# DeltaNet and SwiGLU on one core: scores leave PSUM through two engines, their mask moves to the unit's slot, and the plan is re-timed

## The chip, the core and the metric

The kernel runs on one core of a Trainium2 chip. A core has a matrix engine (TensorE, PE in the profile, with its weight loads shown as PEld), a vector engine (VectorE, DVE), a scalar engine (ScalarE, ACT), GpSimd (POOL) and SyncE (SP), which here only issues DMAs. Each engine takes its instructions strictly in the order of the program; engines wait for each other, and for DMAs, on semaphores. Matmul results land in PSUM, from which only DVE and ACT read here. The metric is the time of one execution on the device in microseconds, and the time before is the median of four runs.

## The reference: what is computed

Two blocks follow each other. The first is a DeltaNet recurrence over 768 steps for 4 batches of 8 heads with head dimension 48; the second is an RMS norm and a SwiGLU feed-forward block over the 3,072 resulting tokens, with 384 model columns and 1,536 hidden columns:

```python
k_n = k / (np.linalg.norm(k, axis=-1, keepdims=True) + 1e-06)
for t in range(S):
    y[:, :, t] = np.einsum('bhd,bhde->bhe', q[:, :, t], state)
    v_old = np.einsum('bhde,bhd->bhe', state, kt)
    state = state + bt[:, :, :, None] * np.einsum('bhd,bhe->bhde', kt, vt - v_old)
...
rms = np.sqrt(np.mean(x * x, axis=-1, keepdims=True) + 1e-06)
xn = x / rms * rms_g
g = xn @ w_gate
silu = g * (1.0 / (1.0 + np.exp(-g)))
val = xn @ w_val
return (silu * val @ w_out).astype(np.float32)
```

Within a chunk of 128 steps the recurrence becomes a triangular system: scores of keys against keys, and of keys against queries (masked to the earlier steps), an inverse of a unit triangular matrix, and products with the state. The weights arrive as 64-bit floats and the kernel makes 32-bit floats of them itself.

## The kernel before, in words

**Units.** A unit `n` is one chunk of 128 steps of one batch with its 8 heads: 6 chunks by 4 batches give 24 units, units 0 to 3 being chunk 0. The FFN works on pairs of units, 256 tokens, in a pass (`ffn`, L1018) of 12 steps; a step multiplies gate and value (`p_gv`, L1037), takes `sil` on ACT (L1046) and `h_f` on DVE (L1049), and `leave` (L1022) adds the step's product to the output accumulators `p_o` (L1024). The first two pairs run as four half passes of 6 steps.

**The start.** `begin` (L1087) loads keys and queries, scores the keys of chunk 0 (`score_part`, `keep_keys`), sends the diagonal 32 by 32 blocks through DRAM into the layout of the inversion (`gather_two`, tile `gd`, then `gblk`), scores the queries (the Q phase), and inverts on DVE (`invert_halves`). The result goes through DRAM again (`td`, then `tt`). `stay_warm` issues matmuls whose result nobody reads. `fetch` loads one tile of weights (two DMAs), `shrink` and `convert` (ACT L251; DVE L261 to L292) turn weight tiles into 32-bit floats, five DVE steps for each of 18 tiles; `convert_rest` spreads what is left over the first FFN passes.

**Chunks 1 to 5.** `prepare(n)` normalizes the keys, transposes queries and keys on PE, copies them out (`kqt`, ACT L408), scores both (`score`, L411, four PSUM tiles `p_g`), evacuates the scores into `gp`, and sends the diagonal blocks to DRAM (`gather`, L445). Each of the four `p_g` tiles is evacuated by two ACT copies (`keys`, L428 and L429) and two DVE multiplications by the causal mask (`queries`, L433); both engines write into the same `gp` rows, and the DVE of a tile stands behind its ACT copies. `invert(g)` (L599) runs 31 steps of two DVE instructions (L618, L627) over a chunk or a pair of units. `slot(v, z, y)` (L965) runs the products of up to three units at different stages: `corner`, `inner`, `outer`, `scale`, `transpose_y`.

**PSUM.** Eight buffers: two for `p_gv`, two for `p_o` and the filler, and four (`ps_delta`, L76) that everything else takes in turn. A transpose or a score right behind a score therefore waits until a `p_g` tile is evacuated.

**Order.** There is no automatic scheduler: pieces are generators that yield plan times, `run_plan` (L1078) always advances the one with the earliest time, and the order of the calls is the order on every engine's queue. One plan unit is half an FFN step on PE (6 of the traced matmuls, 1.3 us). The plan's constants stand at the end (L1134 to L1162). SP's queue holds most loads and the output; ACT's queue holds the gathers of `gd`, so that ACT does nothing else while a gather waits for `gp`. `scale_v` multiplies the values of a unit by the key norms on GpSimd.

## Time and profile before

| | before |
|---|---|
| median of 4 runs (lowest to highest) | 857.9 us (854.65 to 859.13) |
| the profiled execution, its time | 859.13 us |
| its span, first to last instruction | 857.4 us |
| PE / DVE / ACT / POOL busy in the span | 816.3 / 497.9 / 247.7 / 111.9 us |
| granted TensorE clock, mean | 0.974 |

The profiled execution is the slowest of the four. The span is cut below into five stretches by what PE does: up to 40.66 us the start, to 67.61 us chunk 0 alone, to 201.9 us the first FFN steps with weight conversion, preparation and inversion of chunk 1, to 342 us chunk 1's slots and chunk 2's inversion, and from there the steady part, in which PE is never without work. A busy PE is a modelled figure: a matmul at half clock counts as busy too.

### The profile page before, as it was taken

Reading aid. Unit: us, or ns where it says so; the run is one execution under the profiler, and the core shown is the slowest. Engines: PE = TensorE matmul, PEld = TensorE weight load, DVE = VectorE, ACT = ScalarE, POOL = GpSimd, SP = SyncE. Lnnn points to the kernel's source line nnn. Section 1 sums busy time; section 2 is a strip of 40 time slices with the busy share of each in tenths; the row PEclk is TensorE's granted clock in tenths of the full one; section 3 lists DMA queues with packets and bytes.
Section 4 is the critical chain, followed back from the end, with each engine's and each line's share of the span. In section 5 each row is a group of like instructions: output and inputs, shape, how many; then the busy total and the mean of one; then the engine's idle time right before and its main releaser. Section 6 shows DMA issues by size and latency. Waiting matters only on the chain.

```text
span 857.4 us, 20449 instructions
## 1 busy us (share of the span) xinstructions
PE 816.3 (95%) x8628; PEld 629.3 (73%) x8628; DVE 497.9 (58%) x1233; ACT 247.7 (29%) x655; POOL 111.9 (13%) x154
## 2 busy tenths in 40 slices
PE   7898978889999989999999999999999999999998
PEld 6586756666777766777778777777778777877776
DVE  7868968793344865755856756856756841211100
ACT  5333545201443141233132142142142121220101
POOL 6003332200113020020020020020020000000000
PEclk9959989899999999999999999999999999999999
DMA  6846335104232042133042051051032020000000
GB/s 153 233 101 222 114 109 162 36 0 105 49 69 65 1 101 48 21 69 75 2 89 55 2 105 39 2 105 40 9 79 39 2 63 1 2 20 1 19 1 18
DMA packets 152204, 52.03 MB, mean 61 GB/s; under 512 B 143760, under 2 KB 146832, under 8 KB 152112
## 3 DMA queue, kind: packets, MB, share of 16 engines
q1 hardware_dynamic: 124960, 36.95, 18.9%
q0 software_dynamic: 2080, 10.23, 3.4%
q10 hardware_dynamic: 25072, 3.54, 2.5%
q8 instruction: 68, 1.11, 0.5%
q14 instruction: 24, 0.20, 0.1%
HBM read 36.54 MB, written 14.16 MB: 59 GB/s over the span
## 4 chain that ended last, share of the span: by engine, by line
PE 68%; DVE 7%; DMA 2%; ACT 2%; SPq 1%; issue 1%; ACTq 1%; DVEq 0%
PE p_gv L1037 36%; PE p_o L1024 18%; DVE tmp L618 3%; DVE ttb L627 2%; PE p_y L781 2%; PE p_g L419 2%; PE p_k L819 2%; PE p_y L819 2%; PE p_z L841 2%; PE p_t L403 1%; DMA gblk<-gd 1%; PE p_v L688 1%; DMA gd<-gp 1%; DVE h_f L1049 1%; ACT gp L428 1%
## 5 line engine op out<-in xcount | busy, mean ns | idle before, releaser
L1037 PE MATMUL p_gv<-xt,wgv_sb 128*128 128x256 f32 x1728 | 414.2, 386 | 1.3 <-DVE xt L1008 0.7
L1037 PEld LDWEIGHTS p_gv<-xt,wgv_sb 128*128 128x128 f32 x1728 | 322.7, 192 | 64.1 <-issue 4.0
L1024 PE MATMUL p_o<-wo_sb,h_f 128*128 128x384 f32 x576 | 215.8, 499 | 9.6 <-DVE h_f L1049 9.5
L1024 PEld LDWEIGHTS p_o<-wo_sb,h_f 128*128 128x128 f32 x576 | 107.6, 193 | 61.0 <-DVE h_f L1049 14.0
L1046 ACT ACTIVATE sil<-p_gv 128x256 f32<-128x256 f32 x144 | 55.2, 383 | 336.1 <-PE p_gv L1037 316.5
L1049 DVE TENSOR_TENSOR h_f<-sil,p_gv 128x256 f32<-128x256 f32 x144 | 60.0, 417 | 153.2 <-ACT sil L1046 152.0
L618 DVE SCALAR_TENSOR_TENSOR tmp<-gblk,nbeta,ttb 64x112 f32<-64x112 f32 (+27 forms) x248 | 101.2, 408 | 29.5 <-DMA gblk<-gd 21.7
L627 DVE TENSOR_TENSOR ttb<-ttb,tmp 64x112 f32<-64x112 f32 (+27 forms) x248 | 86.6, 349 | 8.5
L433 DVE TENSOR_TENSOR gp<-p_g,mask 64x128 f32<-64x128 f32 (+1 forms) x160 | 37.9, 277 | 47.3 <-ACT gp L429 43.2
L993 POOL TENSOR_SCALAR ms<-ms 128x1 f32<-128x1 f32 x24 | 6.2, 259 | 447.0 <-ACT y L985 446.7
L338 POOL TENSOR_TENSOR knrm<-ksum,half 128x8 f32<-128x8 f32 x24 | 41.2, 1717 | 166.2 <-DVE ksum L337 166.0
L408 ACT COPY kqt<-p_t 128x512 f32<-128x512 f32 x48 | 28.0, 584 | 41.0 <-PE p_t L403 29.1
L419 PE MATMUL p_g<-kqt 64*64 64x192 f32 x640 | 32.1, 329 | 4.4 <-ACT kqt L408 2.4
L841 PEld LDWEIGHTS p_z<-v_raw,tt 64*64 64x64 f32 x768 | 25.9, 142 | 9.4 <-issue 6.8
L419 PEld LDWEIGHTS p_g<-kqt 64*64 64x64 f32 x640 | 22.7, 132 | 13.6 <-issue 5.9
L985 ACT ACTIVATE y<-p_y 128x384 f32<-128x384 f32 x24 | 11.8, 490 | 67.6 <-PE p_y L781 67.6
L841 PE MATMUL p_z<-v_raw,tt 64*64 64x48 f32 x768 | 28.8, 227 | 1.4 <-ACT sil L1046 1.4
L708 ACT COPY vs<-p_v 32x256 f32<-32x256 f32 x48 | 17.4, 362 | 42.2 <-PE p_w L695 37.9
L859 PE MATMUL p_x<-tt,gp 64*64 64x64 f32 x384 | 28.8, 229 | 0.0
L781 PE MATMUL p_y<-u,gp 128*64 128x48 f32 x768 | 27.7, 229 | 0.0
L781 PEld LDWEIGHTS p_y<-u,gp 128*64 128x64 f32 x768 | 26.4, 145 | 1.4 <-issue 1.4
L428 ACT COPY gp<-p_g 128x128 f32<-128x128 f32 x80 | 21.2, 265 | 16.1 <-PE p_g L419 14.5
(128 smaller groups left out, 808.7 us busy)
## 6 DMA issues: line engine op xcount, KB each, us to landing
kpad<-in_k_dram SPq DMA_DIRECT2D x24, 192.0 KB, 2.8
qpad<-in_q_dram SPq DMA_DIRECT2D x24, 192.0 KB, 3.2
v_raw<-in_v_dram SPq DMA_DIRECT2D x24, 192.0 KB, 3.6
out_dram<-o_sb SPq DMA_DIRECT2D x24, 192.0 KB, 2.0
raw<-in_moe_w_val_dram POOLq DMA_DIRECT2D x8, 384.0 KB, 4.0
raw<-in_moe_w_out_dram POOLq DMA_DIRECT2D x8, 384.0 KB, 4.1
gd<-gp ACTq DMA_DIRECT2D x80, 32.0 KB, 2.1
tt<-td SPq DMA_DIRECT2D x80, 32.0 KB, 2.1
```

The lines of the kernel that those rows point to most:

```text
L338: nc.gpsimd.tensor_tensor(out=norms[c][:, b * H : (b + 1) * H], in0=ksum, in1=half, op=ALU.pow)
L419: nc.tensor.matmul(to, pair[d, K1 if i else K0], pair[d, places], skip_group_check=True)
L433: nc.vector.tensor_tensor(out=to[p, :, place], in0=p_g[p, :, place], in1=mask[p, i, None].to_broadcast([p.stop, 2, HC]), op=ALU.mult,)
L618: nc.vector.scalar_tensor_tensor(out=tmp, in0=gblk[p, i, None, i + 1 :].to_broadcast(shape), scalar=nbeta[p, i : i + 1], in1=ttb[p, 0 : i ...
L627: nc.vector.tensor_tensor(out=to, in0=to, in1=tmp, op=ALU.add)
L781: nc.tensor.matmul(p_y[p, h], gp[i][:, h, HC * place : HC * (place + 1)], u[:, h], start=(n_y < B and h == 0), stop=True, skip_group_check ...
L819: nc.tensor.matmul(p_o[p, 2 * j : 2 * j + 2].rearrange("p h d -> p (h d)"), kq[:, j, place], st[:, j], start=(alone or j == 0), stop=alone ...
L841: nc.tensor.matmul(p_z[p, h], tt[n_z % B][p, h], r[p, h], start=(h == 0), stop=(p is lo or n_z >= B), skip_group_check=True,)
L1024: nc.tensor.matmul(p_o[i], h_f[:, i * C : (i + 1) * C], wo_sb[:, f], start=(f == f0), stop=(f == f1 - 1),)
L1037: nc.tensor.matmul(p_gv[:, i], wgv_sb[:, i * KT + t, f * 128 : (f + 1) * 128], xt[:, t], start=(t == 0), stop=(t == KT - 1),)
L1046: nc.scalar.activation(out=sil, in_=p_gv[:, 0], func=ACTF.Silu)
L1049: nc.vector.tensor_tensor(out=h_f, in0=sil, in1=p_gv[:, 1], op=ALU.mult)
```

## The change

- **Scores.** `score` no longer takes an evacuation function. Each `p_g` tile is emptied by one engine alone with two plain copies (`leave`, 64 partitions by 384 numbers): the tiles of heads 0 to 3 by ACT, those of heads 4 to 7 by DVE, alternating. No mask is applied there.
- **Mask.** `mask_queries(n)` (two DVE instructions on `gp`, 64 by 512) now runs for every unit, in `slot` after `corner`; for units 2 and 3 it moves from the start of `first_chunk` to behind `inner`.
- **Blocks.** The 80 gathers of `gd` in `gather` are issued by SP instead of ACT.
- **Values.** `scale_v` for units 2 and 3 and for chunk 1 runs on ACT as 8 multiplications for each unit, at the unit's slot; chunk 2 and later stay on GpSimd.
- **Start.** In `begin`, the key norm's DVE part comes after the key copies, unit 3's copies are all on ACT, the first `shrink` and `convert` move into the Q phase behind its first transpose, and one weight tile fewer is fetched there; it is fetched behind `read_two(0)`.
- **FFN pass ends.** The last `leave` of a pass is yielded 2.5 plan units later instead of 0.9, behind the first matmuls of the next pass.
- **Other.** `transpose_y` of units 2 and 3 leaves PSUM through ACT (three multiplications) instead of DVE (one), `norm_k` in `prepare` moves one yield later, and the plan's times are re-set: preparation of chunk 1 from 8 + 4.5 b to 12.4 + 3.4 b with shorter yields, `invert(1)` from 33.5 with 0.62 a step to 30.4 with 0.68, slots 0.7 to 3 units later, `invert(2)` with 0.7 a step instead of 0.58.

```diff
@@ -385,6 +385,10 @@
 
     def scale_v(n, engine=nc.gpsimd):
         c, b = divmod(n, B)
+        if engine is nc.scalar:
+            for h in range(H):
+                nc.scalar.mul(vraw[n][:, h], vraw[n][:, h], norms[c][:, b * H + h : b * H + h + 1])
+            return
         engine.tensor_tensor(
             out=vraw[n],
             in0=vraw[n],
@@ -407,8 +411,12 @@
             )
         nc.scalar.copy(kqt[place_of(n)][:, :, place::2], p_t)
 
-
-    def score(n, groups, evacuate):
+    def leave(to, p_g, copy):
+        copy(out=to[lo, :, Q0:K1], in_=p_g[lo, :, Q0:K1])
+        copy(out=to[hi, :, K0:], in_=p_g[hi, :, K0:])
+
+
+    def score(n, groups):
         b = place_of(n)
         p_gs = [[ps_delta([128, 2, 4, HC], "p_g") for par in range(2)] for g in range(NP // 2)]
         for j in range(NP):
@@ -419,27 +427,10 @@
                 nc.tensor.matmul(
                     to, pair[d, K1 if i else K0], pair[d, places], skip_group_check=True
                 )
-        for g in range(NP // 2):
-            for par in range(2):
+        for par in range(2):
+            for g in range(NP // 2):
                 to = gp[b][:, 4 * g + par : 4 * g + 4 : 2].rearrange("p h (a t) -> p h a t", a=4)
-                evacuate(to, p_gs[g][par])
-
-    def keys(to, p_g):
-        nc.scalar.copy(to[:, :, K0], p_g[:, :, K0])
-        nc.scalar.copy(to[hi, :, K1], p_g[hi, :, K1])
-
-    def queries(to, p_g):
-        for place, p, i in ((Q0, lo, 0), (Q1, slice(0, C), 1)):
-            nc.vector.tensor_tensor(
-                out=to[p, :, place],
-                in0=p_g[p, :, place],
-                in1=mask[p, i, None].to_broadcast([p.stop, 2, HC]),
-                op=ALU.mult,
-            )
-
-    def both(to, p_g):
-        keys(to, p_g)
-        queries(to, p_g)
+                leave(to, p_gs[g][par], nc.vector.tensor_copy if g else nc.scalar.copy)
 
 
     def gather(n, size):
@@ -448,7 +439,7 @@
             gds[n // size] = dram.tile([NBLK * size * H, W, W], FP32, name=f"gd{size}")
         for a in range(NBLK):
             o, first = diagonal(a), (a * size + i) * H
-            nc.scalar.dma_start(
+            nc.sync.dma_start(
                 out=gds[n // size][first : first + H].rearrange("h r j -> r h j"),
                 in_=gp[place_of(n)][W * a : W * (a + 1), :, o : o + W],
             )
@@ -481,15 +472,16 @@
         return [(0, a), (1, b), (0, b), (1, a)]
 
     def prepare(n, size, dts):
-        norm_k(n, square_k(n, nc.scalar))
+        ksq = square_k(n, nc.scalar)
         yield dts[0]
+        norm_k(n, ksq)
         transpose(n, qpad[n % 2], Q0)
         if n + 2 < NU:
             load_q(n + 2)
         yield dts[1]
         transpose(n, kpad[n % NK], K0)
         yield dts[2]
-        score(n, crossed((0, slice(0, 3)), (1, slice(1, 4))), both)
+        score(n, crossed((0, slice(0, 3)), (1, slice(1, 4))))
         yield dts[3]
         gather(n, size)
         if n % size == size - 1:
@@ -518,11 +510,11 @@
     def heads(n, par, place):
         return gp[n][:, par::2, HC * place : HC * (place + 1)]
 
-    def keep_keys(n, p_gs):
+    def keep_keys(n, p_gs, copy=nc.vector.tensor_copy):
         for par in range(2):
             nc.scalar.copy(heads(n, par, K0)[lo], p_gs[par][lo, :, 0])
             own = gp[n][hi, par::2].rearrange("p h (a t) -> p h a t", a=4)
-            nc.vector.tensor_copy(out=own[:, :, K0::2], in_=p_gs[par][hi])
+            copy(out=own[:, :, K0::2], in_=p_gs[par][hi])
 
     def keep_queries(n, p_gs):
         for par in range(2):
@@ -531,7 +523,7 @@
 
     def mask_queries(n):
         for place, p in ((Q0, lo), (Q1, hi)):
-            part = gp[n][p, :, HC * place : HC * (place + 1)]
+            part = gp[place_of(n)][p, :, HC * place : HC * (place + 1)]
             nc.vector.tensor_tensor(
                 out=part, in0=part, in1=mask[p, place // 2, None].to_broadcast([HC, H, HC]), op=ALU.mult
             )
@@ -603,7 +595,7 @@
         if size == B:
             yield 1.5
             turn_beta(g)
-            for n in range(B * g, B * (g + 1)):
+            for n in range(B * g, B * (g + 1)) if g > 1 else ():
                 scale_v(n)
         else:
             apart = split_beta(g)
@@ -919,15 +911,12 @@
         yield
         update(0)
         load_k(B + 1)
-        scale_v(2)
-        scale_v(3)
-        mask_queries(2)
         yield dt
         update(1)
         reload()
         yield dt
         next(halved[2])
-        mask_queries(3)
+        scale_v(2, nc.scalar)
         yield dt
         next(halved[3])
         yield dt
@@ -935,6 +924,7 @@
         yield dt
         corner(2, None)
         next(halved[3])
+        scale_v(3, nc.scalar)
         yield dt
         corner(3, 2)
         yield dt
@@ -944,16 +934,18 @@
         inner(2, None, 3)
         yield dt
         inner(3, 2, None)
+        mask_queries(2)
         yield dt
         outer(None, 2)
         yield dt
         inner(None, 3, None)
+        mask_queries(3)
         yield dt
         outer(None, 3)
         yield dt
-        transpose_y(2, scale(*ys.pop(2)))
-        yield dt
-        transpose_y(3, scale(*ys.pop(3)))
+        transpose_y(2, scale(*ys.pop(2)), nc.scalar)
+        yield dt
+        transpose_y(3, scale(*ys.pop(3)), nc.scalar)
         yield dt
         update(2)
         yield dt
@@ -963,10 +955,12 @@
 
 
     def slot(v, z, y, dts):
-        if have(v) and v >= 3 * B:
-            scale_v(v)
+        if have(v) and not 2 * B <= v < 3 * B:
+            scale_v(v, nc.scalar if v < 2 * B else nc.gpsimd)
         if have(v) or have(z):
             corner(v, z)
+        if have(v):
+            mask_queries(v)
         yield dts[0]
         inner(z, y, z)
         yield dts[1]
@@ -998,19 +992,21 @@
         nc.scalar.mul(y, p_y.rearrange("p h d -> p (h d)"), rs)
         return y
 
-    def transpose_y(n, y):
+    def transpose_y(n, y, engine=nc.vector):
         if n % 2 == 0:
             xts[n // 2] = work.tile([128, KT, TOK], FP32, name="xt")
         o = C * (n % 2)
         p_xt = ps_delta([128, KT, 128], "p_xt")
         for t in range(KT):
             nc.tensor.transpose(p_xt[:, t], y[:, t * 128 : (t + 1) * 128], ident)
-        nc.vector.tensor_tensor(
-            out=xts[n // 2][:, :, o : o + C],
-            in0=p_xt,
-            in1=g_sb[:, :, None].to_broadcast([128, KT, 128]),
-            op=ALU.mult,
-        )
+        xt = xts[n // 2][:, :, o : o + C]
+        if engine is nc.scalar:
+            for t in range(KT):
+                nc.scalar.mul(xt[:, t], p_xt[:, t], g_sb[:, t : t + 1])
+        else:
+            nc.vector.tensor_tensor(
+                out=xt, in0=p_xt, in1=g_sb[:, :, None].to_broadcast([128, KT, 128]), op=ALU.mult
+            )
 
     halves = {}
 
@@ -1051,7 +1047,8 @@
                 leave(f - 1, last)
                 yield 1
             last = h_f
-        yield 0.9
+
+        yield 2.5
         leave(f1 - 1, last)
         for i in range(2):
             n = 2 * m + i
@@ -1091,16 +1088,16 @@
         transpose(0, kpad[0], K0)
         for n in range(B):
             if n + 1 < B:
-                norm_k(n + 1, square_k(n + 1, nc.vector))
+                ksq = square_k(n + 1, nc.vector)
                 transpose(n + 1, kpad[n + 1], K0)
             if n == 2:
                 gather_two(0)
                 turn_all_beta()
-            keep_keys(n, score_part(n, K0))
+            keep_keys(n, score_part(n, K0), nc.scalar.copy if n == 3 else nc.vector.tensor_copy)
+            if n + 1 < B:
+                norm_k(n + 1, ksq)
         gather_two(2)
         scale_beta(0, B)
-        tops.append(shrink(raws[0]))
-        convert(2)
         clear_ttb()
         for t in state + [ne]:
             nc.gpsimd.memset(t, 0.0)
@@ -1110,9 +1107,12 @@
                 turn_beta(0)
                 convert(3)
             transpose(n, qpad[n % 2], Q0)
+            if n == 0:
+                tops.append(shrink(raws[0]))
+                convert(2)
             stay_warm(2)
             load_q(n + 2)
-            if n < 3:
+            if n < 2:
                 fetch(nc.sync.dma_start)
             if n < 2:
                 load_v(n)
@@ -1120,6 +1120,7 @@
         tops.append(shrink(raws[1]))
         inverses = invert_halves()
         read_two(0, *inverses)
+        fetch(nc.sync.dma_start)
         stay_warm(4)
         stay_warm(8, ttb_all[:, 0:DM].rearrange("p (t m) -> p t m", m=128))
         mask_queries(0)
@@ -1136,32 +1137,32 @@
         at(18 * i, ffn(m, half_f * (i // 2), half_f * (i // 2 + 1)))
     at(0, convert_rest(0.5))
     for b in range(B):
-        at(8 + 4.5 * b, prepare(B + b, B, (4, 3, 1.5, 1.8)))
-    at(33.5, invert(1, B, 0.62, 0.62))
+        at(12.4 + 3.4 * b, prepare(B + b, B, (2.5, 1.6, 1.6, 1.5)))
+    at(30.4, invert(1, B, 0.68, 2.2))
     for g in range(B // 2):
         at(72 + 36 * g, ffn(B // 2 + g, 0, FT))
 
-    for i, begin_i in enumerate((57, 59.7, 62.4, 65, 71, 78)):
+    for i, begin_i in enumerate((57.7, 60.4, 63.1, 65.8, 72, 79)):
         n = B + i
         own = (x if B <= x < 2 * B else None for x in (n, n - 1, n - 2))
         at(begin_i, slot(*own, (1, 1, 1, 1) if i < 4 else (1.2, 1.2, 1.2, 1)))
-    begins = {2 * B: 109, 2 * B + 1: 115.5, 2 * B + 2: 122}
+    begins = {2 * B: 112, 2 * B + 1: 118, 2 * B + 2: 124, 3 * B: 151}
     for n in range(2 * B, NU + 2):
         begins.setdefault(n, 18 * (n - 3) - 15)
         own = (x if 2 * B <= x < NU else None for x in (n, n - 1, n - 2))
         at(begins[n], slot(*own, (2, 2.5, 2, 1.5)))
     for b in range(B):
-        at(64 + 4.7 * b, prepare(2 * B + b, B, (1.4, 1.2, 1.4, 1.8)))
-    at(84, invert(2, B, 0.58, 2))
+        at(65 + 4.4 * b, prepare(2 * B + b, B, (1.4, 1.2, 1.4, 1.8)))
+    at(84.2, invert(2, B, 0.7, 1.8))
     for g in range(3 * B // 2, NU // 2):
-        start = begins[2 * g - 3] + 8.6 if 2 * g - 3 > 2 * B + 1 else 100
+        start = begins[2 * g - 3] + 8.6 if 2 * g - 3 > 2 * B + 1 else 106
         for x in range(2):
             at(start + 3.6 * x, prepare(2 * g + x, 2, (1.4, 1.2, 1.4, 1.8)))
         at(start + 9.6, invert(g, 2, 0.84, 1.7))
     for g in range(B, NU // 2):
         at(36 * g, ffn(g, 0, FT))
     with tc.manual_schedule():
-        first = first_chunk(1.2, begin())
+        first = first_chunk(1.12, begin())
         next(first)
         at(1, first)
         run_plan()
```

## Prediction

> **What bounds the kernel now.** I read the stretches first, then the waits of PE and DVE, then single gaps in time order. Columns of the stretches: PE, PEld, DVE, ACT, POOL busy, granted clock, DMA share.
>
> ```profile
> 0.00:40.66 40.66, 32.26 (x356) 22.67 (x357) 33.60 (x84) 17.82 (x39) 13.35 (x20) 0.96 0.81 203
> 40.66:67.61 26.95, 26.12 (x466) 22.72 (x466) 15.22 (x28) 9.66 (x24) 4.86 (x10) 0.62 0.46 101
> 67.61:201.90 134.29, 115.41 (x999) 85.33 (x1000) 111.42 (x223) 46.65 (x112) 29.37 (x39) 0.92 0.37 110
> 201.90:342.00 140.10, 131.38 (x1616) 99.40 (x1616) 72.92 (x211) 45.41 (x128) 18.49 (x22) 1.00 0.27 56
> 342.00:857.40 515.40, 511.13 (x5194) 399.13 (x5192) 264.75 (x690) 128.14 (x352) 45.87 (x64) 1.00 0.17 36
> ```
>
> From 342 us PE is full (511.13 of 515.40, and most of the rest is the output after the last matmul), so what happens there costs nothing unless it makes a new gap. What can be won lies before: PE idles 18.9 us in the third stretch and 8.7 in the fourth, and 8.4 in the first. In the third, DVE is busy 111.4 of 134.3 us: weight conversion, then 31 inversion steps, in a fixed order. That queue sets when chunk 1's slots can start; PE has work for 115 us there, part of it at half clock. The waits of DVE in that stretch, and of PE from there to 342 us (total, times, longest):
>
> ```profile
> DVE h_f L1049 <- ACT sil L1046: 7.6, 5, 2.6
> DVE gp L433 <- ACT gp L429: 5.0, 4, 1.9
> DVE xt L1008 <- PE p_xt L1007: 2.3, 1, 2.3
> DVE tmp L618 <- POOL ttb L544: 1.5, 1, 1.5
> DVE ksum L335 <- ACT ksq L325: 0.9, 1, 0.9
> ...
> PE p_o L1024 <- DVE h_f L1049: 8.6, 5, 2.9
> PE p_t L403 <- DVE gp L433: 4.4, 2, 3.0
> PE p_g L419 <- ACT kqt L408: 2.4, 1, 2.4
> ```
>
> The gaps in time order (start, length, idle before and releaser):
>
> ```profile
> 40.66 2.46 PE L739 MATMUL p_vh<-tt,gp 64*64 64x32 f32 x63 [2.54 <-DMA tt<-td]
> ...
> 143.80 0.63 PE L403 MATMUL p_t<-ident,qpad 128*128 128x128 f32 x4 [2.98 <-DVE gp L433]
> ...
> 163.54 2.93 PE L1024 MATMUL p_o<-wo_sb,h_f 128*128 128x384 f32 x4 [2.90 <-DVE h_f L1049]
> ...
> 192.68 2.93 PE L1024 MATMUL p_o<-wo_sb,h_f 128*128 128x384 f32 x4 [2.69 <-DVE h_f L1049]
> ...
> 307.97 0.63 PE L403 MATMUL p_t<-ident,qpad 128*128 128x128 f32 x4 [1.41 <-DVE gp L433]
> ...
> 312.73 1.53 PE L419 MATMUL p_g<-kqt 64*64 64x192 f32 x32 [2.40 <-ACT kqt L408]
> ```
>
> At 143.80 ACT had emptied its part of the scores by 142.45, but DVE, behind conversion, began its masks at 143.07, and the transpose needs the bank. At 163.54 and 192.68 a pass end waits for `h_f` with no other matmul in front. At 312.73 `kqt` stood behind gathers in ACT's queue. At 40.66 the inverse of chunk 0 comes late: `td` is issued at 32.20 and lands at 36.98, 4.8 us, while the row of that DMA has a median of 3.2.
>
> **The change part by part.**
>
> **Start.** The Q phase fetches one tile (two DMAs of 384 KB) less; in the DMA order they stand right before the last queries and `td`. I take `td` at the row's median: 4.8 - 3.2 = 1.6 us earlier (bounds: 0, if the rest of the queue still holds it, and 2.1, down to the 2.7 of the next inversion's `td`). Against it: `ksum` of unit 3 now follows `keep_keys`, so its GpSimd power (1.6 us) ends near 16.7 instead of 14.8 and `scale_beta` a microsecond later; but DVE then waits no longer for `shrink` (0.84), and the inversion starts within 0.2 us of before. Unit 3's copies on ACT and the PE gap of 3.36 us at 18.02 don't lie on this path, which is DVE. The moved fetch now stands before four `ne` reads on SP, needed only for units 2 and 3. Sum: -1.4.
>
> **Third stretch, DVE's queue.** I added DVE's instructions from the first `h_f` to the first inversion step in both orders, by their rows: about 77 us in each, so the work isn't less; only waits can go.
> - Scores: before, 8 DVE multiplications (0.277) and 8 ACT copies (0.26) for each unit, one behind the other; after, 4 and 4 of 384 numbers. No row has that shape: DVE lies between 0.352 (192 numbers from PSUM) and 0.691 (512), I take 0.55; ACT between 0.37 (256) and 0.59 (512), I take 0.48. So 2.2 us against 2.2 on DVE, 1.9 against 2.1 on ACT: nothing. What goes is DVE waiting for ACT, 5.0 us; it still waits for PE to score, I keep half: -2.5 (bounds 0 and -5.0).
> - `xt` of units 2 and 3 leaves DVE: 2.3 us of waiting and 2 x 0.556 of work: -3.4. Late next is PE: `p_xt` now stands close behind `sil` and `y`, 0.38 + 0.58 on ACT, some 1 us twice; that is PE idle, not DVE.
> - `ksum` no longer follows its square at once: -0.9. In the new order the clearing of `ttb` stands ahead of GpSimd's two memsets that waited for the end of conversion: -1.5.
> - Values of chunk 1 off GpSimd: the four inversion steps beside them took 0.75 to 0.78 us each, the next four 0.25 to 0.34; four times 0.5 is -2.0.
> - DVE waiting for `sil`: some of it follows PE gaps (2.59 us at 127.68, after 4.4 us of PE gaps around 116, whose scores now come after both `p_xt`; 1.39 after the gap of 143.80). Half: -2.5 of 5.1 us (the rest of 7.6 lies after the inversion).
> - Pass ends 2.5 units later put 12 matmuls (2.6 us) in front of the last `leave`, as much as the 2.90 and 2.69 us waited. DVE stays as late as it was, so this moves PE's work but not DVE's path: 0 here, up to -5.6 if PE were the path. The next pass's `p_o` comes 2.5 units later still, beyond two 0.48 us copies.
> - Masks of units 4 to 7 leave this stretch, but the copies stay, so that is counted above.
>
> The sum is -12.8. A tighter queue waits in new places, and 0.68 a step instead of 0.62 stretches 31 steps by 1.9 units (2.4 us) if DVE then gets ahead of its plan. I take -10 (bounds -2 and -17, all DVE waits plus contention).
>
> **Fourth stretch.** The gathers leave ACT: its waits on them are 11.4 + 4.2 + 2.2 us over the run, but only the 2.40 at 312.73 reached PE. The 1.41 at 307.97 goes as the first bank is now ACT's alone. New: each slot has 2 masks on DVE (0.682 each, 1.4 us a unit; 20 units, 27 us) and the first ones 8 multiplications on ACT. For one, bounds: 0.19 (accumulator read, 128x1) and 0.58 (`y`, 128x384); I take 0.30, nearer the 0.256 of a 16x128 copy: 2.4 us a unit. ACT is idle 3.5 and 3.9 us ahead of the copies at 207.77 and 214.87, and DVE 5.2, 2.6 and 4.2 us at 207.17, 210.34 and 217.44, which hides them; at the fourth slot only 2.0 us. I put 0.8 on PE's path. Sum: -3.8 + 0.8 = -3.0 (bounds -8.7 and +5).
>
> The Trainium skill, "ScalarE: Activation LUTs", section "Rules for kernel authors", says to do multiplications on VectorE and not on ScalarE, and speaks against this part; by its figure for a pointer operand (280 ns + 0.833 per element, estimate 0.32 us, 2.6 us a unit) six units cost ACT 15 us. If all of that were on the path the sum would be about even; the idle rows above say it isn't.
>
> **SP.** It takes 80 issues of 0.31 to 0.51 us, some 36 us in a queue with long idle times. A gather now holds SP until both engines have emptied `gp`; behind it stand query loads for units two or more later, then `gblk`, which needs the gather anyway. 0, up to 3 us if a load is late.
>
> **Steady part.** 0, with cover: between `corner` and `inner` the plan puts 2 units, 2.6 us of matmuls. If that cover were gone, 16 units' masks would cost 22 us.
>
> **Clock.** The clock record grants half from 18.6, 42.5, 117.6, 144.9, 162.0 and 192.7 us, for 3.4 to 20.5 us, each after PE idled; fewer gaps may spare some of the last four. On DVE's path that is no gain. The skill's "TensorE: Matmul & The Clock Gate", section "Why this matters for your kernels", warns of idle gaps over about 3 us; the drops here follow gaps of 2.54 and of 1.25 with 1.23 us. By the rule only the longest gaps would matter.
>
> **Sum.** -1.4 - 10 - 3.0 = -14.4 from the profiled execution's 859.1: 844.7. This execution is the slowest of the four and 1.2 above the median of 857.9; I predict **844**.
>
> **The rivals.**
> - **More goes**: PE is more often the path than I say, and the pass ends and half clocks count too. Of 18.9 + 8.7 us idle three quarters go, 20.7, with 1.4 and some 5 of half clock (163.54: 2.93 instead of the 1.49 of a `leave` elsewhere): 832. For it: gaps end on different engines. Against it: DVE's 77 us stay.
> - **About the same**: DVE's waits turn into others (`sil`, PE), the third stretch gives nothing, the others -1.4 - 3: 855. For it: DVE's work isn't less. Decides if DVE then idles 20 us as before.
> - **Slower**: masks stand in DVE's queue before `inner`'s `u`, on every slot. 20 units x 1.4 = 27 us; exposed in full, 844.7 + 27 = 872. From 862.2 up it is slower, so 17.5 of the 27 us must be exposed. Against it: DVE is busy only 264.75 of 515.40 us in the steady part.
>
> **How the numbers follow.** Likeliest 0.55 (838 to 851), more goes 0.24, about the same 0.12, slower 0.09. A measurement of this kernel tells about 0.5% from no change. Faster by more, below 853.6: 0.55 + 0.24 and a little of the third, 0.80; within: 0.11; slower: 0.09. The range 831 to 857 leaves out the lower half of the second and all of the last.
>
> **What would show it.** Right: the first slot's `corner` near 190 instead of 201.9 us; no DVE wait on ACT at the score copies; steps of about 0.2 to 0.3 us at the start of the inversion; no PE gap over 2 us after 45 us; `p_vh` near 39. Wrong: DVE idle in the third stretch still near 20 us, PE waiting for `v_raw`, `tt` or `gp` in slots, or PE idle after 342 us.

## The result and the profile after

The changed kernel takes 854.6 us (median of 43 executions, 850.01 to 857.15). The kernel before, run many more times beside it, takes 854.78 us (64 executions, 850.47 to 861.88), not the 857.9 of the first four. The ratio is 0.9993, 95% interval 0.9981 to 1.0004: no change. Forecast were 844 us and a gain.

The two profiled executions mislead: before's took 859.13 us, 4.3 above its median, after's 851.04, 3.6 below its own. Single executions of one kernel spread over some 10 us, and the spread goes with the clock granted to TensorE (last section), so below times are medians and profiles are used for places and waits.

The stretches of the changed kernel, cut at the same events as before's (inverse of chunk 0 read, first `xt`, first slot's corner, 342 us); columns are PE, PEld, DVE, ACT, POOL busy, granted clock, DMA share, GB/s:

```profile
0.00:39.17 39.17, 32.58 (x357) 22.20 (x357) 30.86 (x80) 19.10 (x41) 14.25 (x20) 0.96 0.77 187
39.17:64.06 24.89, 20.81 (x466) 17.40 (x466) 16.61 (x30) 9.76 (x24) 6.18 (x12) 0.86 0.62 151
64.06:187.15 123.09, 109.03 (x998) 82.38 (x999) 110.95 (x207) 52.73 (x126) 23.23 (x32) 0.97 0.39 116
187.15:342.00 154.85, 147.34 (x1859) 112.14 (x1860) 87.63 (x208) 52.79 (x137) 18.45 (x23) 0.99 0.25 54
342.00:849.30 507.30, 499.61 (x4951) 389.55 (x4949) 280.99 (x667) 122.75 (x303) 45.77 (x64) 0.99 0.17 36
```

The third stretch is 123.1 us long instead of 134.3, with the same PE instructions in it (998 against 999) and DVE as busy as before (110.95 against 111.42 us): DVE idles 12.1 us where it idled 22.9. That is what was forecast for this stretch; but PE's busy time is shorter too, 109.03 instead of 115.41 us, with more clock granted (0.97 instead of 0.92). And from the corner to the end the kernel now needs 662.2 us, before 655.5, and the last stretch, which was full, has PE idle 7.7 us. The waits of PE (total, times, longest) and its three long gaps (start, length, idle before and releaser) say where:

```profile
PE p_nb L363 <- DVE beta_t L355: 6.3, 3, 4.7
PE p_o L1020 <- DVE h_f L1045: 6.2, 3, 4.3
PE p_v L680 <- DMA tt<-td: 3.7, 2, 3.1
PE p_xt L1001 <- ACT y L992: 3.5, 3, 1.3
```

```profile
148.46 0.33 PE L363 MATMUL p_nb<-ident,beta_t 32*32 32x32 f32 x8 [4.71 <-DVE beta_t L355]
...
187.15 0.22 PE L680 MATMUL p_v<-tt,gp 32*32 32x32 f32 x2 [3.05 <-DMA tt<-td]
...
391.75 1.01 PE L1020 MATMUL p_o<-wo_sb,h_f 128*128 128x384 f32 x1 [4.28 <-DVE h_f L1045]
```

The gaps of before at 143.80, 163.54, 192.68, 307.97 and 312.73 us are gone, and these came: PE idle (span less busy) is 41.1 us before and 39.9 after. The third one is new in kind, since it lies in the full part. Its cause stands in SP's queue (SPq, the DMA issues of SyncE) and then in DVE's:

```profile
371.62 0.45 SPq L622 DMA_DIRECT2D td<-ttb  x1
373.56 0.45 SPq L631 DMA_DIRECT2D nd<-gblk  x1
374.50 1.85 SPq L636 DMA_DIRECT2D tt<-td  x4
376.45 0.90 SPq L642 DMA_DIRECT2D ne<-nd  x2
377.39 1.93 SPq L636 DMA_DIRECT2D tt<-td  x4
379.37 0.94 SPq L642 DMA_DIRECT2D ne<-nd  x2
380.41 0.87 SPq L1066 DMA_DIRECT2D out_dram<-o_sb  x2
381.38 2.95 SPq L442 DMA_DIRECT2D gd<-gp  x4
385.73 0.47 SPq L447 DMA_DIRECT2D gblk<-gd  x1
```

```profile
378.67 0.20 DVE L384 TENSOR_SCALAR nbeta<-p_nb 64x32 f32<-64x32 f32 x1 [0.69 <-PE p_nb L381]
389.35 0.25 DVE L610 SCALAR_TENSOR_TENSOR tmp<-gblk,nbeta,ttb 64x31 f32<-64x31 f32 x1 [10.49 <-DMA gblk<-gd]
389.64 0.19 DVE L619 TENSOR_TENSOR ttb<-ttb,tmp 64x31 f32<-64x31 f32 x1
389.86 1.39 DVE L527 TENSOR_TENSOR gp<-gp,mask 64x512 f32<-64x512 f32 x2
391.28 0.42 DVE L1045 TENSOR_TENSOR h_f<-sil,p_gv 128x256 f32<-128x256 f32 x1
```

The second unit's gather stands behind twelve reads of the previous inverse and two output writes, some 0.45 us of SP each, although the unit's scores were all in `gp` at 375.8 us. So `gblk` is issued at 385.73, DVE waits 10.49 us for it, and behind that wait stand the slot's masks, which are new there, and an `h_f` that PE needs: 4.28 us of idle PE, and the clock record grants half from 390.7 us on for 6.8 us.

### The profile page after: what moved, and what is told of

Its sections match the earlier page's. It is cut to its first block, busy times and chain, and to the rows that moved or that the text cites. A ratio compares the mean times of both kernels' runs of the same rounds, so it can differ in the third digit from the quotient of the medians.

```text
span 849.3 us, 20329 instructions
## 1 busy us (share of the span) xinstructions
PE 809.4 (95%) x8628; PEld 623.7 (73%) x8628; DVE 527.0 (62%) x1189; ACT 257.1 (30%) x631; POOL 107.9 (13%) x148
## 4 chain that ended last, share of the span: by engine, by line
PE 77%; DVE 10%; DMA 4%; ACT 3%; issue 2%; SPq 1%; DVEq 0%; ACTq 0%
PE p_gv L1033 39%; PE p_o L1020 19%; PE p_g L427 3%; PE p_y L773 2%; PE p_z L833 2%; PE p_k L811 2%; DVE tmp L610 2%; PE p_y L811 2%; PE p_t L407 2%; DVE ttb L619 1%; PE p_v L680 1%; PE p_xt L1001 1%; PE p_x L851 1%; PE p_s L792 1%; PE p_w L687 1%
## 5 line engine op out<-in xcount | busy, mean ns | idle before, releaser
L610 DVE SCALAR_TENSOR_TENSOR tmp<-gblk,nbeta,ttb 64x112 f32<-64x112 f32 (+27 forms) x248 | 100.2, 404 | 32.5 <-DMA gblk<-gd 26.3
L415 DVE COPY gp<-p_g 64x384 f32<-64x384 f32 x40 | 22.0, 549 | 41.8 <-PE p_g L427 41.2
L833 PEld LDWEIGHTS p_z<-v_raw,tt 64*64 64x64 f32 x768 | 26.3, 142 | 11.3 <-issue 7.0
L527 DVE TENSOR_TENSOR gp<-gp,mask 64x512 f32<-64x512 f32 x48 | 32.8, 683 | 0.5
L851 PEld LDWEIGHTS p_x<-tt,gp 64*64 64x64 f32 x384 | 25.5, 142 | 2.3 <-ACT tt L702 1.6
```

Source lines behind the costliest of these rows:

```text
L610: nc.vector.scalar_tensor_tensor(out=tmp, in0=gblk[p, i, None, i + 1 :].to_broadcast(shape), scalar=nbeta[p, i : i + 1], in1=ttb[p, 0 : i ...
L833: nc.tensor.matmul(p_z[p, h], tt[n_z % B][p, h], r[p, h], start=(h == 0), stop=(p is lo or n_z >= B), skip_group_check=True,)
L851: nc.tensor.matmul(p_x[lo, h], gp[place_of(n_x)][hi, h, HC * K0 : HC * (K0 + 1)], tt[n_x % B][hi, h], skip_group_check=True,)
```

## The experiments

Ratios are to the kernel before on the same chip in the same group of runs, with 95% intervals. "First slot" is the time from `p_vh` (inverse of chunk 0 read) to unit 4's corner, "rest" from there to the end of the span, both from one profile. Two profiles of one kernel differ by up to 3.3 us in the one and 0.8 in the other; after_gather_pair_act, whose program is after's up to some 370 us, has 153.1 us to the first slot where after has 148.0 and 149.3. So a difference under some 5 us in "first slot" says little by itself. Names with `ga_` are the changed kernel with its gathers on ScalarE and what the name says.

| kernel | median us | ratio | PE idle | `p_vh` | first slot | rest |
|---|---|---|---|---|---|---|
| before | 854.8 | 1 | 41.1 | 40.66 | 161.2 | 655.5 |
| before_again | 855.9 | 1.0012 [0.9984, 1.0039] | 42.6 | 39.61 | 158.0 | 655.1 |
| after | 854.6 | 0.9993 [0.9981, 1.0004] | 39.9 | 39.17 | 148.0 | 662.2 |
| after_again | 857.5 | 1.0012 [0.9990, 1.0035] | 41.8 | 39.72 | 149.3 | 662.8 |
| after_gather_act | 847.4 | 0.9895 [0.9865, 0.9925] | 35.8 | 41.11 | 147.1 | 658.2 |
| ga_again | 847.3 | 0.9923 [0.9907, 0.9938] | 35.8 | 40.95 | 149.6 | 657.5 |
| after_gather_pair_act | 847.5 | 0.9920 [0.9898, 0.9943] | 36.7 | 40.64 | 153.1 | 654.6 |
| before_gather_sp | 861.1 | 1.0081 [1.0053, 1.0109] | 44.3 | 39.33 | 157.7 | 660.8 |
| ga_pass_early | 855.4 | 1.0047 [1.0025, 1.0068] | 42.9 | 39.60 | 151.6 | 661.7 |
| ga_mask_early | 858.1 | 1.0065 [1.0040, 1.0091] | 45.3 | 39.37 | 153.7 | 661.2 |
| ga_scale_v_pool | 845.3 | 0.9917 [0.9894, 0.9941] | 36.7 | 39.40 | 150.7 | 653.6 |
| ga_old_plan | 847.3 | 0.9937 [0.9914, 0.9960] | 34.0 | 41.71 | 152.0 | 653.0 |
| ga_xt_dve | 848.4 | 0.9926 [0.9904, 0.9948] | 37.4 | 40.05 | 149.9 | 655.9 |
| before_pass_late | 855.0 | 1.0008 [0.9992, 1.0024] | 39.1 | 39.79 | 157.8 | 654.6 |
| before_mask_slot | 860.4 | 1.0076 [1.0047, 1.0104] | 45.0 | 41.23 | 160.6 | 658.6 |
| before_mask_pass | 856.0 | 1.0011 [0.9989, 1.0034] | 39.6 | 39.93 | 159.0 | 655.5 |
| before_mask_pass_xt | 856.4 | 1.0015 [0.9984, 1.0046] | 40.4 | 41.44 | 158.3 | 655.5 |

### Both kernels once more

> The kernel before, unchanged, profiled once more, to see how much of the 8.1 us between the two profiled executions (859.1 before, 851.0 after) belongs to the kernels. Theory A (most of it is the granted clock of that one execution): the PE gaps over 0.25 us again add up to about 35.7 us and stand at the same places, but the stretches at half clock differ in place and length, the granted clock is nearer 0.98 than 0.974, and the time is 852 to 857. Rival B (the order of the kernel before fixes its clock): half clock again from 42.5 to 63 us and at 117, 145, 162 and 193, some 60 us in all, clock 0.974, time near 858.

> The changed kernel, unchanged, profiled once more. Theory A: gaps over 0.25 us again near 35.6 us, with the gap of some 4 us at 391 and of some 3 us at 187 in place, but more time at half clock than the 27 us of the first profile, and a time of 853 to 857. Rival B: again clock 0.983 and 851.

The places hold: gaps over 0.25 us add up to 37.4 us in the kernel before (35.7 in the first profile) at nearly the same points, and the changed kernel again waits 4.72 us at 150, 3.10 at 189 and 4.79 at 395 us. The half clocks don't hold: before's from 42.5 to 63 us is 13.7 us long here instead of 20.5, and those at 145 are gone; the clock is 0.984. So rival B is out for the kernel before, and 4.6 of the 8.1 us between the first two profiles were before's execution, not its order. For the changed kernel both expected times missed in part: this profile had 0.984 and 853.6, the other nine executions 854.5 to 860.0.

### The gathers on ScalarE again, and on SyncE alone

```diff
-            nc.sync.dma_start(
+            nc.scalar.dma_start(
                 out=gds[n // size][first : first + H].rearrange("h r j -> r h j"),
```

> The changed kernel with one part undone: a unit's four gather transfers are issued by ScalarE again, not by SyncE. Theory A (the second pair unit's gather stands on SyncE's queue behind the reads of the inverse before it and costs PE 4.3 us of idle time at 391 plus half of 6.8 us at half clock): DVE's wait of 10.5 us for the block at 379 to 389 falls to about what it was before (the sum of these waits from 26.3 to about 22 us), the PE gap at 391 goes, and the time falls by 4 to 7 us, to about 848 to 851. Rival C (the gathers on ScalarE delay its other work by as much, as the 2.4 us gap at 312 of the kernel before): the gap at 391 goes, others of the same size come at 310 to 330, and the time is within 1.5 us of 854.6.

> The kernel before with one part of the change alone: the gathers on SyncE. Theory A: the gap of 2.4 us at 312 goes, and a gap of some 4 us appears where a pair's second gather stands behind the reads of an inverse (near 390 to 410 us): 2 to 5 us slower, 857 to 860. The step of the prediction that put this at 0 would be confirmed by a time within 1.5 us of 854.8; a gain of 2 us or more would say that ScalarE's waits on the gathers cost more than the one gap.

> The changed kernel with the gathers issued by ScalarE, once more, to be the base beside the others of this group and to see whether the 8.6 us hold on another chip. Theory A (SyncE's queue cost the change its whole gain): 846 to 849, 0.6 to 1.2% below the kernel before, PE idle (span less PE busy) near 36 us where both given kernels have 40 to 42.

One word takes 0.8 to 1.05% off the changed kernel, on two chips, and puts 0.8% on the kernel before. In both the part after the corner moves by some 5 us (662.5 to 657.9, and 655.3 to 660.8). On ScalarE the second gather goes out at 377.81 us, beside SP's reads, and DVE's queue of after_gather_act has at this place:

```profile
382.22 0.20 DVE L384 TENSOR_SCALAR nbeta<-p_nb 64x32 f32<-64x32 f32 x1
388.62 0.25 DVE L610 SCALAR_TENSOR_TENSOR tmp<-gblk,nbeta,ttb 64x31 f32<-64x31 f32 x1 [6.21 <-DMA gblk<-gd]
...
390.54 0.42 DVE L1045 TENSOR_TENSOR h_f<-sil,p_gv 128x256 f32<-128x256 f32 x1
```

The longest wait for `gblk` falls from 10.49 to 6.21 us (all of them from 26.3 to 19.1), and PE waits 0.85 us there. `gblk` itself is still issued on SP at 384.44, behind the reads. The gap at 312 of the kernel before doesn't return, so rival C falls. The profiles show less of the cost than the medians do: 851.04 and 853.58 us against 848.25 and 849.82, PE idle after 342 us 7.7 and 8.2 us against 4.6 and 4.7. The rest of the 7 to 9 us isn't located in them; the median granted clock is 0.976 with the gathers on SyncE and 0.985 or 0.986 with them on ScalarE, while the changed kernel's two profiled executions had 0.983 and 0.984. In before_gather_sp the same jam comes earlier, at another pair, where DVE's wait was 9.5 us in the kernel before; DVE's waits from 310 to 345 us and PE's gap:

```profile
DVE tmp L618 <- DMA gblk<-gd: 15.7, 1, 15.7
```

```profile
331.63 0.31 PE L841 MATMUL p_z<-v_raw,tt 64*64 64x48 f32 x1 [7.52 <-issue]
```

The profile names no releaser for this gap ("issue"); but the `v_raw` that the matmul reads is written by DVE at 330.99 us, in its queue right behind the wait for `gblk`.

### Only the paired units' gathers on ScalarE

```diff
-            nc.sync.dma_start(
+            (nc.sync if size == B else nc.scalar).dma_start(
```

> The changed kernel with the gathers on ScalarE only for the units inverted two at a time (from unit 12 on), on SyncE for chunks 1 and 2. Theory A (the cost is the second pair unit's gather behind the reads of the inverse before it): the whole gain, 845 to 849. Rival (the gathers of chunks 1 and 2 on SyncE cost as well): between, 849 to 853.

847.5 us, 0.9920 [0.9898, 0.9943]: the whole gain. The gathers of chunks 1 and 2 cost nothing on SP that could be measured; the price is that of units inverted two at a time, where a gather follows at once on the inverse before.

### One part undone, with the gathers on ScalarE

Later pass ends undone:

```diff
-        yield 2.5
+        yield 0.9
         leave(f1 - 1, last)
```

> From here on the base is the changed kernel with its gathers issued by ScalarE (847.4 us), and one more part is undone in each run. Here the last two matmuls of a pass come 0.9 units after the last h_f again, not 2.5. Theory A (the step of the prediction: DVE's queue is the path, PE's order at a pass end is worth 0): 847.4 within 1.5 us, with gaps of 2 to 3 us at the pass ends and a smaller gap at 188. Rival D (PE is the path there): two gaps of 2.7 to 2.9 us return near 160 and 190, with 3.4 us at half clock each, and the time is 5 to 9 us longer, 852 to 856.

Rival D: 8 us slower by the medians, 1.2 to 1.5% by the ratios. The waits of 2.7 to 2.9 us don't come back (the longest for `h_f` is 1.5), but there are ten of them, 6.6 us in all, and PE idles 8.2 us after 342 us where it idled 4.6.

Masks right behind the score copies:

```diff
         score(n, crossed((0, slice(0, 3)), (1, slice(1, 4))))
+        mask_queries(n)
         yield dts[3]
...
-        if have(v):
-            mask_queries(v)
```

> The masks of a unit right behind its score copies again (still two instructions in place, 1.4 us of DVE a unit), not in its slot. Theory A (every us of DVE's queue before chunk 1's inversion moves the first slot and the end): 4 units x 1.4 = 5.5 us on the path, gap at 188 near 8 us, 851 to 854. Rival D: the masks fall into DVE's waits, or PE has other work, and the time is 847.4 within 1.5 us; it may even be shorter, since the small PE waits on masks in slots (1.1 us) go.

More than theory A: 858.1 us. Up to the first slot DVE is busy some 6 us longer (131.8 us against 125.6 and 126.1), as four times 1.4 says, and the slot comes 5.3 us later (148.3, the mean of the two bases, to 153.7), which by itself is only the spread of the profiles; the rest is 3.3 us longer.

Values of chunk 1 on GpSimd:

```diff
-            for n in range(B * g, B * (g + 1)) if g > 1 else ():
+            for n in range(B * g, B * (g + 1)) if g > 0 else ():
...
-        if have(v) and not 2 * B <= v < 3 * B:
-            scale_v(v, nc.scalar if v < 2 * B else nc.gpsimd)
+        if have(v) and v >= 3 * B:
+            scale_v(v)
```

> The values of chunk 1 multiplied by GpSimd again, beside the first inversion steps, not by ScalarE in the slots. Theory A (the step of the prediction: four inversion steps 0.5 us slower each, 2.0 us on DVE's path, 0.8 us less in the slots): +1.2 us, about 848.6, the first steps at 0.75 us again. Rival D (ScalarE's eight multiplications a unit hold back the copies to tt, PE waits of 0.6 and 0.3 us at 200 to 217): these waits go and the time is 1 to 2 us shorter.

Rival D has the mechanism: the waits for ScalarE's `tt` at 200 to 217 us are gone, and PE idles 4.5 us from the corner to 342 us instead of 7.1 and 7.5. Theory A's sign failed: the first inversion steps take 0.24 and 0.19 us here too, since GpSimd now multiplies at 148.5 to 152.4 us, before the inversion begins (158.43). Beside it two steps of the weight conversion take 1.63 and 1.47 us instead of 0.96, which is 1.2 us on DVE's queue; that the first slot is 2.4 us later lies within the spread. The net, 845.3 against 847.3, is 2 us, less than the intervals of the two ratios can tell apart.

The plan's times of the kernel before (all of them up to the last FFN passes), and `xt` of units 2 and 3 on VectorE:

```diff
-        at(12.4 + 3.4 * b, prepare(B + b, B, (2.5, 1.6, 1.6, 1.5)))
-    at(30.4, invert(1, B, 0.68, 2.2))
+        at(8 + 4.5 * b, prepare(B + b, B, (4, 3, 1.5, 1.8)))
+    at(33.5, invert(1, B, 0.62, 0.62))
...
```

```diff
-        transpose_y(2, scale(*ys.pop(2)), nc.scalar)
+        transpose_y(2, scale(*ys.pop(2)))
...
-        transpose_y(3, scale(*ys.pop(3)), nc.scalar)
+        transpose_y(3, scale(*ys.pop(3)))
```

> The plan's times of the kernel before (units of chunk 1 from 8 in steps of 4.5, inversion at 33.5 with 0.62 a step, slots from 57, later ones likewise) with all else of the changed kernel. Theory A (the instructions that went are what counts, the times only have to fit): 847.4 within 2 us. Rival E (the times carry the gain): most of the 8.6 us is lost, 853 to 858, with PE gaps at other places: the inversion begins later against the FFN matmuls in front and the first slot's corner comes late.

> The changed kernel with gathers on ScalarE and xt of units 2 and 3 on VectorE again. Theory A (the step of the prediction, 3.4 us on DVE's path): 849 to 852. Rival D (two PE gaps of 1.0 and 1.2 us at 108 and 112 that wait for ScalarE's y go, and VectorE's wait is filled by other work): 846 to 848.

Neither moves the time by what can be measured (847.3 and 848.4). The new times of the plan carry nothing by themselves, and the `xt` step shows 1 of its 3.4 us, less than the intervals can tell from nothing; the first slot (149.9 against 148.3 us) doesn't tell more.

### One part alone in the kernel before

The later pass ends (as above, the other way round), then the score copies in halves with the masks in the slot (functions `leave`, `score`, `mask_queries` and `slot` of the changed kernel), then both, then both with `xt` on ScalarE:

```diff
-        yield 0.9
+        yield 2.5
```

```diff
-                evacuate(to, p_gs[g][par])
+                leave(to, p_gs[g][par], nc.vector.tensor_copy if g else nc.scalar.copy)
...
             corner(v, z)
+        if have(v):
+            mask_queries(v)
         yield dts[0]
```

> The kernel before with one part alone: the last two matmuls of a pass 2.5 units behind the last h_f, not 0.9. Theory F (PE itself was the path at the pass ends; putting this at 0 was an error): the gaps of 2.9 and 2.7 us near 160 and 190 go with their half clocks, and the time falls 4 to 8 us, to about 0.992 of before. Theory A (DVE's queue is the path): the idle time moves to the first slot's corner, a gap of 4 to 6 us there, and the time stays within 1.5 us.

> The kernel before with one part alone: scores copied half by ScalarE, half by VectorE, and masked in the unit's slot. Theory A (the step of the prediction, DVE waits on ScalarE and masks leave the stretch before the inversion): the gaps of 3.0 us near 142 and 1.4 near 303 go, DVE reaches chunk 1's inversion 3 to 5 us earlier, and the time falls by 3 to 6 us. Rival (masks in the slots stand before u): up to 22 us more; any time above the kernel before speaks for it. If undoing a part in the changed kernel costs more than the same part alone brings here, the parts only work together.

> The kernel before with two parts together: masks in the slots (alone: 6 us slower) and the pass ends 2.5 units later (alone: no change). Theory G (the two need each other: masks in a slot make h_f late at the pass ends, 4 us of PE idle after 342 us, and the later pass end hides that, while the masks gone from the stretch before the inversion then show): 848 to 852, PE idle after 342 us back at about 1 us. Rival H (the gain of the changed kernel with gathers on ScalarE comes from its other parts: start, values, xt, order of ksum): 853 to 858.

> The kernel before with three parts: masks in the slots, pass ends 2.5 units later, and xt of units 2 and 3 on ScalarE. The two parts without the third left 856.0, with VectorE's waits of 1.7 us on p_xt at 117 and 3.6 us on sil at 127 in its queue. Theory I (with these two parts in, the xt step of 3.4 us on VectorE's path is real in the plan of the kernel before, and only in the new plan, where the units of chunk 1 are scored at other times, is it worth nothing): 849 to 852, the wait on sil at 127 gone, the first slot's corner 3 to 5 us earlier than 199. Rival (the missing gain is in ksum's order, the values off GpSimd or the start): 854 to 857.

The pass ends alone do about what theory A said: the gap of 2.9 us near 160 shrinks to 2.3, that near 190 goes, and the corner waits 3.44 us instead of 0.8 to 1.2. The masks in the slots alone cost 0.76%, and from 342 us on they show in the stretch and in the waits of PE:

```profile
342.00:860.40 518.40, 510.03 (x5128) 398.09 (x5126) 286.74 (x678) 125.60 (x312) 45.86 (x64) 1.00 0.17 35
```

```profile
PE p_o L1014 <- DVE h_f L1039: 2.7, 5, 0.5
PE p_nb L381 <- DVE apart L370: 2.3, 5, 0.5
```

With the later pass ends as well the same stretch is idle 4.1 us instead of 8.4:

```profile
342.00:854.40 512.40, 508.34 (x5125) 397.87 (x5123) 286.30 (x677) 125.44 (x310) 45.95 (x64) 1.00 0.17 36
```

So the later pass end pays for the masks in the slots, as theory G had it; but there is no gain beyond that, neither with two parts nor with `xt` as the third. Theories G and I both fall on their times, and their rivals have them right without saying which other part it is. What the three parts lack stands in DVE's waits from 100 to 165 us, first before_mask_pass_xt, then ga_old_plan, which has the same plan and all parts:

```profile
DVE gp L412 <- PE p_g L424: 6.2, 2, 3.3
DVE ksum L335 <- ACT ksq L325: 4.5, 2, 3.6
DVE h_f L1041 <- ACT sil L1038: 2.7, 1, 2.7
```

```profile
DVE gp L415 <- PE p_g L427: 4.6, 2, 2.7
DVE tmp L610 <- POOL ttb L536: 1.5, 1, 1.5
```

With `xt` on ScalarE the sum over `ksq` waits for the square behind it, 4.5 us; in the changed kernel `norm_k` comes a step later. That reading is argued from the waits: `ksum`'s order was not run alone, and neither were the start and units 2 and 3's masks and values. Which of them completes the gain stays open.

### Versions that beat both

The prediction held that DVE's queue is the path to the first slot. Each of these has the gathers on ScalarE and the values of chunk 1 on GpSimd. best1 (first diff) moves plan times, best2 (second) takes work off DVE, best3 is best2 with the third:

```diff
-    at(30.4, invert(1, B, 0.68, 2.2))
+    at(31.6, invert(1, B, 0.68, 2.2))
...
-    for i, begin_i in enumerate((57.7, 60.4, 63.1, 65.8, 72, 79)):
+    for i, begin_i in enumerate((59.7, 62.4, 65.1, 67.8, 73, 79)):
```

```diff
-                leave(to, p_gs[g][par], nc.vector.tensor_copy if g else nc.scalar.copy)
+                leave(to, p_gs[g][par], nc.vector.tensor_copy if g and n >= 2 * B else nc.scalar.copy)
```

```diff
-    for i, begin_i in enumerate((57.7, 60.4, 63.1, 65.8, 72, 79)):
+    for i, begin_i in enumerate((59.3, 62, 64.7, 67.4, 72.8, 79)):
```

> A version meant to be better than both: gathers on ScalarE, values of chunk 1 on GpSimd, and in the plan the inversion of chunk 1 1.2 units later and its slots 2 units later (the last two 1 and 0), so that FFN matmuls stand where PE waits 4.7 us for beta and 3 us for the inverse. Theory A (PE is idle there only because the FFN matmuls stand behind the waiting ones): gaps at 150 and 190 shrink by 3 us or more together, time 841 to 844. Rival (DVE's chain is the path, the idle time only moves behind the slots): 845 to 848, with a gap at the first FFN matmul of the next pair near 225.

> Meant to be better than both: gathers on ScalarE, values of chunk 1 on GpSimd, and the score copies of chunk 1 all on ScalarE, so that VectorE has 16 copies of 0.55 us less (8.9 us with their waits of 2.7 us less) ahead of chunk 1's inversion. Theory A (VectorE's queue is the path up to the first slot's corner): corner 4 to 7 us earlier and 840 to 843. Rival (ScalarE's copies then come one behind the other and the transposes and silu behind them wait): 844 to 850.

> The version of 842.4 us (gathers on ScalarE, chunk 1's values on GpSimd, its score copies on ScalarE) with chunk 1's slots 1.6 units later in the plan (the fifth 0.8), so that some 3 us of FFN matmuls stand ahead of the corner that waits 4.2 us for the inverse. Theory J (that idle time is only a matter of order): gap below 1.5 us, 838.5 to 841. Rival (the slots' chain is the path to the next pair's FFN): the time moves behind the slots, 842 to 844.

best1: 846.6 us, 0.9915 [0.9888, 0.9943], as ga_scale_v_pool: the wait for beta shrinks to 3.08 us and a wait of 3.15 us for `h_f` stands next to it, the corner still waits 2.35. This later order gained nothing. best2: 842.4 us, 0.9859 [0.9835, 0.9883]; 16 copies fewer on DVE, the gap for beta is gone and the corner comes 144.8 us after `p_vh` instead of 150.7. The time falls by 0.6%, clear of the intervals: DVE's queue was the path there. Then the corner waits for the inverse alone:

```profile
185.27 0.28 PE L680 MATMUL p_v<-tt,gp 32*32 32x32 f32 x2 [3.36 <-DMA tt<-td]
186.34 0.37 PE L680 MATMUL p_v<-tt,gp 32*32 32x32 f32 x6 [0.79 <-DMA tt<-td]
```

best3 lets FFN matmuls in front of it:

```profile
183.56 1.56 PE L1020 MATMUL p_o<-wo_sb,h_f 128*128 128x384 f32 x4 [1.40 <-DVE h_f L1045]
184.96 1.46 PE L1033 MATMUL p_gv<-xt,wgv_sb 128*128 128x256 f32 x6
186.35 0.75 PE L680 MATMUL p_v<-tt,gp 32*32 32x32 f32 x32
```

834.05 us, 0.9742 [0.9703, 0.9781], some 20 us below both kernels and below what was expected. PE idle is 27.2 us instead of best2's 29.2, and PE's busy time fell from 809.8 to 804.9 us with the same work: no half clock is granted after 92.7 us, where best2 had 6.8 us of it at 185.1 and 20.5 instead of 13.7 near 42. The latter lies before the two programs differ, so it belongs to the execution; how much of the 8 us between the medians is order and how much clock stays open.

## Why the prediction was wrong

**The step that failed is "SP: 0, up to 3 us if a load is late".** It counted the issues (36 us in a queue with long idle times) and named loads as the only thing behind a gather. What stands in front of a gather was not counted: twelve reads and two writes, 6.8 us of issues from 374.50 to 381.28, before the gather of a unit whose inversion DVE is about to start. Measured by itself: +0.81% in the kernel before, 0.8 to 1.05% in the changed kernel, 7 to 9 us. That is all that the rest of the change gains: the other steps together brought 7 to 9 us, not 14.4. The sentence that `gblk` "needs the gather anyway" was true and beside the point: both were late together.

**The base.** The sum was made against 859.1 us. This execution lay 4.3 us above what 64 executions have as their median; with that median the same -14.4 would have given 840.4. So the value lay closer than its steps.

**Third stretch, -10: the size came out, its parts did not.** From `p_vh` to the corner it is 148.0, 149.3 and, in after_gather_pair_act, 153.1 us instead of 161.2 and 158.0, on average -9.5. The waits of DVE on ScalarE at the copies are gone, and the first inversion steps take 0.24, 0.19, 0.28 and 0.22 us. But PE's idle time there fell only from 20.8 to 17.7 us on average; the other 6.4 us are PE's busy time for the same work, with 20.5 us at half clock on average instead of 34.1. At the same 27.3 us of half clock before_again needs 158.0 and after_gather_pair_act 153.1. "On DVE's path that is no gain" put this at nothing, and as the median clock of the changed kernel is no higher than that of the kernel before (last section), part of the 9.5 us is the luck of the profiled executions. In the list, `xt`, -3.4, showed 1 us when undone; "pass end 0" cost 8 us of the time when undone, since PE's order there also sets when DVE gets its next `h_f`; "masks leave this stretch, but that is counted above" was 6 us of DVE's work; and the first inversion steps kept their pace with the values on GpSimd. Errors of both signs stand in the list.

**Fourth stretch, -3.0: at most 1 us of PE's idle time.** The gaps at 307.97 and 312.73 went as said, but PE idles 7.5 and 8.5 us from the corner to 342 us, where it idled 8.7 and 8.4. The multiplications on ScalarE, priced at 0.8 us, cost 1.9 us of PE's waits: shorter than taken (0.24 us each, not 0.30) and hidden in ScalarE's idle time, they still hold back its copies to `tt`, and PE waits for these four times. With the times of the old plan (ga_old_plan) the same multiplications cause no such wait, so it takes the plan's new times as well. The Trainium skill's "ScalarE: Activation LUTs", section "Rules for kernel authors", which the prediction set aside on the strength of idle rows, has multiplications done on VectorE. No run here put these on VectorE; off ScalarE, on GpSimd, the waits for `tt` went, and the 2 us that the time fell are within the noise.

**Start, -1.4.** 0. The first profile pair shows 40.66 and 39.17, but seven profiles with the old start have `p_vh` at 39.33 to 41.44, mean 40.3, and thirteen with the new one at 39.17 to 41.71, mean 40.2. One row of one execution was taken for the order's own.

**Steady part, 0.** Right for the masks, and for the reason given only in part: without the later pass ends PE idles 4 us more there (before_mask_slot, ga_pass_early). The cover was the pass end's reserve, not the two units in front of `inner` alone. The gather's jam, which does lie there, was never looked for, since the stretch was taken as closed.

**The rivals.** "About the same" had the right time by another road: its DVE waits did not come back. "Slower through the masks" has its mechanism in before_mask_slot, +0.76%, at a quarter of the price. Of what was to show the steps right, the corner, the inversion's steps and the score copies without a wait on ACT did; "no PE gap over 2 us after 45 us" failed three times, and two signs of being wrong came true: "PE idle after 342 us", and PE waiting for `tt` (3.05 us at the first slot, 1.9 us behind ScalarE's copies).

## What to carry to other kernels

When a DMA issue is moved to another queue, don't count that queue's load; list what stands in front of the moved issue at each place where it will come due, and who waits in order behind its data. An engine with work in fixed order pays at the end only for the path: take work off it first, and only then fill the idle time in front of what waits (best1's later slots alone gained nothing, a like order after best2 gained 1%). Take the base from many executions, not from the profiled one, and undo parts as well as adding them: here two parts, the pass ends and the masks, cost 8 to 11 us when undone and gain nothing when added alone.

## What was not expected of the hardware

The granted clock goes with most of the spread between executions of one kernel. Over the 97 executions of the kernel before that stand beside the experiments, the mean granted clock lies between 0.968 and 0.988 and goes with the time at a correlation of -0.83, 5.5 us for each 0.01: twelve at 0.984 have a mean of 852.2 us, four at 0.972 one of 860.0. The medians follow it: 0.976 for the changed kernel, 0.978 to 0.982 for the kernel before, 0.983 to 0.986 for the three runs of the changed kernel with all or the paired gathers on ScalarE, 0.988 for best3. So PE gaps that go seem to pay twice, in idle time and in clock, and the second price differs from one execution to the next: the same program had 13.7 to 27.3 us at half clock on the way to its first slot. That the gaps set the clock was not tested by itself.

Half clock comes in spans of 3.4, 6.8, 10.2, 13.7, 20.5 and 23.9 us, multiples of 3.4. The Trainium skill's "TensorE: Matmul & The Clock Gate", section "Part 1: The HAM clock gate", describes a free-running window of about 3.4 us whose phase a kernel doesn't set, and that agrees. The page's figure of under 1% of a typical kernel's span is for the warm-up alone. Here the executions at 0.984 and 0.972, half clock in the middle of the kernel included, lie 0.9% apart, as much as a whole part of this change.
